# An attention-and-GEGLU kernel whose plan is made by its own list scheduler: DMA transposes before the normalisation, a model of the VectorE–GpSimd port, and another rule for a spare PSUM bank

## The chip, the cores and the metric

The kernel runs on one core of a Trainium2 chip. The metric is device time in microseconds (us), the median of several executions. Engines are called PE (TensorE; PEld is its weight load), ACT (ScalarE), DVE (VectorE), POOL (GpSimd) and SP (SyncE, which here only issues DMAs).

## The reference

```python
x = A_x                                   # 1 x 2048 x 640, bfloat16
h  = x + attention(layernorm(x))          # 32 heads of 20; one shared K and V head; softmax; output weights
h2 = h + geglu(layernorm(h))              # 640 -> 1536 (gate, up) -> 640, tanh gelu
```

Attention over 2048 keys for 32 heads is 2048 score tiles of 128 keys by 512 query columns, each of which needs an exponential. That is the bulk of the work; the rest ("side jobs") is projections, layer norms and the feed-forward part.

## The kernel before

When the kernel is built, a scheduler in Python (the "planner") simulates the five engines with a modelled cost for every operation, and commits each operation to its engine's in-order stream. On the chip only the order and the semaphores remain. So a modelled cost is not a time; it changes the order.

Score tiles are made four at a time (a "pack"; 512 packs). Each tile sits in one PSUM bank until an exponential has read it. ACT computes most exponentials: one 128x512 instruction for a single tile, or one 128x1024 for a pair in adjacent banks. DVE computes the others with an integer trick: one tensor_scalar from PSUM to `pd`, then two shifted copies, which are integer adds of SBUF data, mostly on POOL. A DVE tile thus needs three P·V matmuls instead of one. For each pack the planner chooses how many of the four tiles, `n`, go to DVE: usually one, sometimes two.

```python
    def score_banks():                       # banks 0..5 are for scores; one of 6, 7 holds the P.V sum,
        res = [0, 1, 2, 3, 4, 5]             # the other serves side jobs
        if spare_ok():
            res += [b for b in (6, 7) if bank_owner[b] is None or bank_owner[b] == "s"]
        return res

    def spare_ok():
        us = open_units()
        if not us or active or any(u["acc"] is None for u in us) or len(us) > 1:
            return False
        if len(us[-1]["left"]) < 3:
            return False
        return not state["misc_ready"]

    # issue_qk: how many tiles of this pack go to VectorE
        elif Dv > TH0:
            n = 0
        elif Dv < TH2 or (SP2 and Dv < SP2D and len(pend[1]) + len(pend[2]) < 2 * SP2P
                          and stall(t, 1, fb) + 1382.0 - stall(t, 2, fb) - 956.0 > SP2G):
            n = 2
        else:
            n = 1
```

`Dv` is the work waiting for DVE. `stall(t, n, fb)` estimates how long ACT will wait for the next pack; it counts the banks that `score_banks()` calls free. The constants 1382 and 956 are ACT's modelled time for a pack with one and with two tiles on DVE: a pair and a single, or two singles.

After each of 32 "units" of attention, the sum is copied to `osb`, transposed by PE with an identity matrix, and normalised by DVE:

```python
    def on_job(u, so):
        ...                                  # four matmuls with the identity into a side bank
        def then(b):
            ...
            dve(lambda e: e.reciprocal(rcp..., v5[:, :, :, Dh]), 200, ...)            # from PSUM
            dve(... e.tensor_tensor(o, v5[:, js, :, 0:Dh], rv..., ALU.mult) ...)      # from PSUM, mostly two of them
```

`plan.commit` knows dependences and engine streams, and nothing of a port that two engines share. Its costs before: 635 ns and 1200 ns for POOL's single and double shift, and 420 ns for the layer-norm scaling (`xn_tmp`) on DVE.

The softmax here doesn't subtract the row's maximum and nothing guards it: scores larger than these inputs give would overflow.

Of the kernel before, what the change touches and what calls it, by code (L numbers as in the profile page):

```python
# [4 lines left out]
ALU = mybir.AluOpType  # L5
# [33 lines left out]
class _Plan:  # L39
# [4 lines left out]
    def __init__(self):  # L44
        self.ops = {e: [] for e in self.ENGINES}
        self.free = {e: 0.0 for e in self.ENGINES}
        self.w = {}
        self.r = {}
# [28 lines left out]
    def commit(self, eng, fn, cost, lat, reads=(), writes=(), at=0.0, dma=False):  # L77
        deps = self._deps(eng, reads, writes)
        t0 = max([self.free[eng], at] + [o.vis for o in deps])
        op = _Op(eng, fn, deps, t0, t0 + cost, t0 + cost + lat, dma)  # L80
# [81 lines left out]
class _Task:  # L162


    __slots__ = ("engs", "fn", "cost", "lat", "reads", "writes", "prio", "then", "gate", "born")

    def __init__(self, engs, fn, cost, lat, reads, writes, prio, then=None, gate=None):
# [8 lines left out]
        self.gate = gate  # L176

# [17 lines left out]
def bass_sequential_preLN__grouped_kv_mqa__glu_gated_geglu__prompt_kernel(  # L195
# [33 lines left out]
    LN2G = CHUNKS  # L229
    PE_T1 = (0, 1)  # L230
    PE_T2 = (15,)
    PE_TO = (15,)
    NA = 16
# [29 lines left out]
    osb = sb("osb", [P, 2, 512], BF16)  # L263
    rcp = sb("rcp", [P, 2, 16], F32)
# [50 lines left out]
    POOL_ADD = 635.0  # L315
    POOL_ADD2 = 1200.0
# [16 lines left out]
    NP0 = 4  # L333
    WQA = 1
# [44 lines left out]
    slots = {"xt": list(range(NXT)), "q": list(range(NQ)), "onT": list(range(4)), "osb": [0, 1], "rcp": [0, 1]}  # L379
# [26 lines left out]
    def ln_group(ln, tiles, prio, done):  # L406
# [27 lines left out]
        def norm(t):  # L434
# [33 lines left out]
            tk = _Task(("dve",), None, 420, L_DVE, keys + [("lr", kk)], [], prio, then, gate)  # L468
# [157 lines left out]
    def on_job(u, so):  # L626
        tl, gs = u["tiles"], u["groups"]
        nt, G = len(tl), len(gs)
        pieces = []
        for j in range(4):  # L630
            pieces.append((mm((lambda j: lambda b: ps[:, b * 512 + j * P:b * 512 + (j + 1) * P])(j),
                              osb[:, so, j * P:(j + 1) * P], ident[:], True, True), c_mm(128),
                           [("osb", so), "ident"]))

        def then(b):
            slots["osb"].append(so)
            sr = slots["rcp"].pop(0)
            v5 = bank(b).rearrange("p (j r e) -> p j r e", j=4, r=4)

            def c1(op):  # L640
                cnt = [0]
                parts = []
                rv = rcp[:, sr, :].rearrange("p (j r) -> p j r", j=4)
                if nt == 4:
                    g = gs[0]
                    o = onq[:, onslot[tl[0]]:onslot[tl[0]] + 4, 4 * Dh * g:4 * Dh * (g + 1)].rearrange(
                        "p j (r d) -> p j r d", r=4)
                    parts.append((o, slice(0, 4)))
                elif nt == 2:
                    for gi, g in enumerate(gs):  # L650
                        o = onq[:, onslot[tl[0]]:onslot[tl[0]] + 2, 4 * Dh * g:4 * Dh * (g + 1)].rearrange(
                            "p j (r d) -> p j r d", r=4)
                        parts.append((o, slice(2 * gi, 2 * gi + 2)))
                else:
                    o = onq[:, onslot[tl[0]], 4 * Dh * gs[0]:4 * Dh * (gs[-1] + 1)].rearrange(
                        "p (j r d) -> p j r d", j=4, r=4)
                    parts.append((o, slice(0, 4)))

                def c2(op):
                    cnt[0] += 1  # L660
                    if cnt[0] == len(parts):
                        free_bank(b)
                        slots["rcp"].append(sr)
                        unit_normed(u)

# [47 lines left out]
    def wo_job(t, s, h):  # L713
# [5 lines left out]
        def then(b):  # L719
# [5 lines left out]
            def fin(op):  # L725
                free_bank(b)
                ln_half(1, t, h, 4.0 if t < 12 else 0.7, ln2_after[t])
# [60 lines left out]
    def gate_job(b, fc):  # L788
# [4 lines left out]
        def then(bk):  # L793
            def fin(op):
# [3 lines left out]
                if gate_left[b] == 0:  # L798
                    gelu(b)
# [922 lines left out]
```

## Time and profile before

| | before |
|---|---|
| median | 804.31 us of three runs; 805.01 over six |
| ACT busy | 750.6 us, 93% |
| exponential tiles on ACT / DVE | 1461 / 587 |
| ACT: exponentials, and its idle time just before them | 699.4 + 26.2 us |

The page's first part of the kernel before: busy time of each engine, share of the span, instructions.

```profile
span 804.6 us, 29858 instructions
## 1 busy us (share of the span) xinstructions
PE 693.7 (86%) x13162; PEld 332.3 (41%) x13162; DVE 627.2 (78%) x1156; ACT 750.6 (93%) x1065; POOL 586.2 (73%) x624
```

ACT is nearest to full. Where it is full shows in the table of stretches (busy us of each engine between two times of the execution, with instruction counts):

```profile
...
core 0: us, PE busy (x) PEld busy (x) DVE busy (x) ACT busy (x) POOL busy (x), PEclk, DMA share, GB/s
0.00:25.00 25.00, 13.13 (x286) 8.26 (x286) 20.03 (x72) 15.48 (x25) 11.94 (x35) 1.00 0.71 174
...
105.00:705.00 600.00, 529.85 (x10345) 250.40 (x10343) 475.08 (x836) 583.96 (x824) 455.26 (x457) 0.97 0.06 13
...
770.00:810.00 40.00, 31.63 (x502) 23.89 (x498) 16.47 (x33) 14.84 (x22) 9.14 (x10) 0.98 0.05 18
```

From 105 to 705 us ACT is busy 583.96 of 600 us. Its idle time lies at both ends.

The groups of instructions that matter (line, engine, operation, output <- input, shapes, count; then busy us and mean ns of one; then idle time of that engine just before them, and what ended it):

```profile
...
L1423 ACT ACTIVATE pa<-ps 128x512 bf16<-128x512 f32 (+1 forms) x1012 | 699.4, 844 | 26.2 <-PE ps L1083 21.5
L1486 POOL TENSOR_TENSOR pd<-pd,shifts 128x512 int32<-128x512 int32 x517 | 534.8, 1043 | 170.5 <-DVE pd L1509 161.1 <-PE ps L510 4.8 <-DVE ln_veb L419 1.4
L1509 DVE TENSOR_SCALAR pd<-ps 128x512 uint16<-128x512 f32 x587 | 395.3, 687 | 142.3 <-PE ps L1083 131.3
...
L1466 DVE TENSOR_SCALAR pd<-pd 128x512 uint16<-128x512 uint16 (+2 forms) x66 | 37.8, 595 | 0.0
...
L472 DVE TENSOR_SCALAR xn_tmp<-xh,mv,ln_r 128x640 bf16<-128x640 bf16 x32 | 21.4, 686 | 0.4
...
L668 DVE TENSOR_TENSOR onq<-ps,rcp 128x160 bf16<-128x160 f32 (+1 forms) x60 | 18.0, 329 | 0.8
...
L674 DVE RECIPROCAL rcp<-ps 128x16 f32<-128x16 f32 x32 | 8.0, 249 | 8.1 <-PE ps L510 6.6 <-PE ps L506 1.3
```

The first line split by form (its busy times add up records that overlap each other):

```profile
...
L1423 ACT ACTIVATE pa<-ps 128x1024 bf16<-128x1024 f32 x449 | 484.7, 1082 | 2.4 <-PE ps L1083 2.3
L1423 ACT ACTIVATE pa<-ps 128x512 bf16<-128x512 f32 x563 | 354.9, 653 | 23.8 <-PE ps L1083 19.2
```

ACT's 1012 instructions cover 1461 tiles, so 699.4 us is 479 ns per tile on average. DVE has room: it sits idle 142.3 us before its exponential tiles. The waits (who waited for whom: us in total, times, longest) show the loop:

```profile
...
PEld ps L1083 <- DVE pd L1509: 161.3, 357, 2.1
POOL pd L1486 <- DVE pd L1509: 161.1, 338, 5.7
DVE pd L1509 <- PE ps L1083: 131.3, 206, 2.5
...
ACT pa L1423 <- PE ps L1083: 21.5, 46, 1.5
```

DVE waits for PE's score matmuls, and the weight loads of score matmuls wait for DVE to give a bank back.

One line from the view of a single source line, for ACT's exponentials (minimum, median and maximum ns; first and last start), is the ruler:

```profile
...
engine op xcount: duration ns min/median/max, first and last start us, forms
L1423 ACT ACTIVATE pa<-ps x1012: 591/756/1242, 14.2 to 777.8; 128x512 bf16<-128x512 f32 x167, 128x1024 bf16<-128x1024 f32 x2
```

The span is 14.2 us before the first exponential, 763.6 us until the last starts, and 804.6 − 777.8 = 26.8 us after that: the tail, which is the feed-forward part of the last rows.

And the same view of the layer-norm scaling:

```profile
...
L472 DVE TENSOR_SCALAR xn_tmp<-xh,mv,ln_r x32: 422/444/1214, 7.1 to 789.1; 128x640 bf16<-128x640 bf16 x32
```

Its median is 444 ns, but some take nearly three times that. The trace shows why: each of the 11 that took over 700 ns and started while a GpSimd operation ran ended 182 to 185 ns after that operation ended, so the long ones had waited it out.

### The profile page before, as it was taken

Reading aid. Unit: us, or ns where it says so; the run is one execution under the profiler, and the core shown is the slowest. Engines: PE = TensorE matmul, PEld = TensorE weight load, DVE = VectorE, ACT = ScalarE, POOL = GpSimd, SP = SyncE. Lnnn points to the kernel's source line nnn. Section 1 sums busy time; section 2 is a strip of 40 time slices with the busy share of each in tenths; the row PEclk is TensorE's granted clock in tenths of the full one; section 3 lists DMA queues with packets and bytes.
Section 4 is the critical chain, followed back from the end, with each engine's and each line's share of the span. In section 5 each row is a group of like instructions: output and inputs, shape, how many; then the busy total and the mean of one; then the engine's idle time right before and its main releaser. Section 6 shows DMA issues by size and latency. Waiting matters only on the chain.

```text
span 804.6 us, 29858 instructions
## 1 busy us (share of the span) xinstructions
PE 693.7 (86%) x13162; PEld 332.3 (41%) x13162; DVE 627.2 (78%) x1156; ACT 750.6 (93%) x1065; POOL 586.2 (73%) x624
## 2 busy tenths in 40 slices
PE   5687778989978998789988799888998899887998
PEld 3332223534434443345433444334444444343457
DVE  7868789877887778877788777988779776877864
ACT  5899999999989999899999999999999999999981
POOL 4587877868767677767878678877777668776760
PEclk9999999989999999999999999999999999998999
DMA  7680001000100000000000000000010000100000
GB/s 198 118 311 2 2 13 24 3 2 2 35 19 3 2 20 18 18 3 3 19 19 18 3 2 19 19 19 2 2 35 19 3 2 19 19 18 11 11 19 18
DMA packets 40288, 21.96 MB, mean 27 GB/s; under 512 B 31328, under 2 KB 38880, under 8 KB 40160
## 3 DMA queue, kind: packets, MB, share of 16 engines
q1 hardware_dynamic: 38848, 19.61, 9.6%
q8 instruction: 105, 1.72, 0.9%
q10 hardware_dynamic: 1312, 0.44, 0.3%
q14 instruction: 23, 0.19, 0.1%
HBM read 10.21 MB, written 2.62 MB: 16 GB/s over the span
## 4 chain that ended last, share of the span: by engine, by line
PE 46%; DVE 25%; ACT 25%; issue 2%; DMA 1%; POOL 1%; POOLq 0%; DVEq 0%
ACT pa L1423 25%; PE ps L510 17%; DVE pd L1509 15%; PE ps L1083 13%; PE ps L1162 13%; DVE pd L1466 3%; PE ps L506 3%; DVE xn_tmp L472 2%; DVE osb L1189 1%; DVE stats L403 1%; DVE qT L580 1%; DVE xh L728 1%; DVE onq L668 1%; DMA onT<-onq 1%; DVE ln_vb L415 0%
## 5 line engine op out<-in xcount | busy, mean ns | idle before, releaser
L1423 ACT ACTIVATE pa<-ps 128x512 bf16<-128x512 f32 (+1 forms) x1012 | 699.4, 844 | 26.2 <-PE ps L1083 21.5
L1486 POOL TENSOR_TENSOR pd<-pd,shifts 128x512 int32<-128x512 int32 x517 | 534.8, 1043 | 170.5 <-DVE pd L1509 161.1
L1509 DVE TENSOR_SCALAR pd<-ps 128x512 uint16<-128x512 f32 x587 | 395.3, 687 | 142.3 <-PE ps L1083 131.3
L1162 PE MATMUL ps<-pd,v_ext 128*32 128x512 bf16 x1761 | 276.2, 400 | 28.0 <-DVE osb L1189 21.5
L1162 PE MATMUL ps<-pa,v_ext 128*32 128x512 bf16 x1461 | 265.4, 393 | 2.7 <-ACT pa L1423 1.3
L1083 PE MATMUL ps<-qT,kT 32*128 32x512 bf16 x2048 | 206.8, 390 | 65.9 <-DVE pd L1509 41.0
L1083 PEld LDWEIGHTS ps<-qT,kT 32*128 32x128 bf16 x2048 | 58.9, 91 | 233.7 <-DVE pd L1509 161.3
L1162 PEld LDWEIGHTS ps<-pd,v_ext 128*32 128x32 bf16 x1761 | 74.8, 98 | 79.1 <-issue 35.0
L1162 PEld LDWEIGHTS ps<-pa,v_ext 128*32 128x32 bf16 x1461 | 70.6, 96 | 43.1 <-issue 30.3
L510 PE MATMUL ps<-xn2T,wg_sb 128*32 128x256 bf16 (+1 forms) x1720 | 66.1, 278 | 0.1
L510 PE MATMUL ps<-xn2T,wu_sb 128*32 128x256 bf16 x1680 | 64.9, 276 | 0.5 <-DVE onq L668 0.4
L510 PE MATMUL ps<-wd_sb,gbuf 128*32 128x320 bf16 x1344 | 64.4, 301 | 0.2 <-DVE onq L668 0.2
L510 PE MATMUL ps<-xn1T,wq_pad 128*32 128x256 bf16 (+1 forms) x1440 | 51.0, 267 | 0.2
L510 PEld LDWEIGHTS ps<-xn2T,wu_sb 128*32 128x32 bf16 x1680 | 42.9, 97 | 18.7 <-issue 10.3
L510 PEld LDWEIGHTS ps<-xn2T,wg_sb 128*32 128x32 bf16 x1720 | 42.1, 98 | 17.6 <-issue 11.5
L510 PEld LDWEIGHTS ps<-wd_sb,gbuf 128*32 128x32 bf16 x1344 | 33.5, 96 | 23.8 <-issue 11.8
L510 PEld LDWEIGHTS ps<-xn1T,wq_pad 128*32 128x32 bf16 x1440 | 33.8, 98 | 13.8 <-issue 8.9
L846 DVE TENSOR_TENSOR gbuf<-ps,gbuf 128x512 bf16<-128x512 f32 x48 | 32.9, 685 | 6.6 <-PE ps L506 6.4
L1466 DVE TENSOR_SCALAR pd<-pd 128x512 uint16<-128x512 uint16 (+2 forms) x66 | 37.8, 595 | 0.0
L1472 POOL TENSOR_TENSOR pd<-pd,shifts 128x256 int32<-128x256 int32 x48 | 30.2, 635 | 3.9 <-DVE pd L1509 3.4
L403 DVE BATCH_NORM_STATS2 stats<-xh 128x6 f32<-128x320 bf16 x64 | 29.9, 477 | 1.3 <-DMA xh<-in_A_x_dram 1.1
L809 DVE CAST gbuf<-ps 128x512 bf16<-128x512 f32 x42 | 28.7, 683 | 1.0 <-PE ps L510 0.9
(71 smaller groups left out, 357.8 us busy)
## 6 DMA issues: line engine op xcount, KB each, us to landing
out_dram<-xh SPq DMA_DIRECT2D x16, 160.0 KB, 1.8
xh<-in_A_x_dram SPq DMA_DIRECT2D x3, 640.0 KB, 6.3
wg_sb<-in_B_w_gate_dram SPq DMA_DIRECT2D x1, 1920.0 KB, 9.3
wu_sb<-in_B_w_up_dram SPq DMA_DIRECT2D x1, 1920.0 KB, 13.6
wd_sb<-in_B_w_down_dram SPq DMA_DIRECT2D x1, 1920.0 KB, 18.0
wo_sb<-in_A_wo_dram SPq DMA_DIRECT2D x1, 800.0 KB, 5.5
gbuf<-in_A_wq_dram ACTq DMA_DIRECT2D x1, 400.0 KB, 4.6
gbuf<-in_A_wq_dram SPq DMA_DIRECT2D x1, 400.0 KB, 6.9
```

The lines of the kernel that those rows point to most:

```text
L403: dve(lambda e: e.bn_stats(stats[:, ln, t, 6 * h:6 * h + 6], xh[:, t, h * HALF:(h + 1) * HALF]), 395, [key], [("st", ln, t, h)], prio, c)
L506: return e.matmul(o(b), l, r, start=st, stop=sp)
L510: ins = e.matmul(o(b)[a, :], l[:, a], r, start=st, stop=sp, tile_position=(0, 32 * j))
L809: dve(lambda e: e.tensor_copy(o, i), c_dve(n * k), [("b", bk)], ks, 1.0, fin)
L846: dve(lambda e: e.tensor_tensor(o, i, o, ALU.mult), c_dve(n * k), [("b", bk)] + ks, ks, 1.0, fin)
L1083: ins = e.matmul(bank(b), kT4[32 * r:32 * r + 32, kt * P:(kt + 1) * P], qT[32 * r:32 * r + 32, s, :], start=True, stop=True, tile_position ...
L1162: ins = e.matmul(ps[32 * r:32 * r + 32, ab * 512:(ab + 1) * 512], v_ext[:, it["kt"], it["w"], :], it["ap"], start=st, stop=(j in ends), ti ...
L1423: op = plan.commit("act", lambda e: e.activation(dst, src, ACT.Exp, scale=SM_SCALE), cost, L_ACT, [("b", b0 + i) for i in range(n)], [("pa ...
L1466: return e.tensor_scalar(pd[:, w, a], pd[:, 0, a], float(CH_SHIFT[w]), None, ALU.add)
L1472: return e.tensor_tensor(pd32[:, w, h], pd32[:, 0, h], shifts[:, w - 1:w].to_broadcast([P, 256 * k]), ALU.add)
L1486: return e.tensor_tensor(pd32[:, 1:3, h], pd32[:, 0, h].unsqueeze(1).to_broadcast([P, 2, 256]), shifts[:].unsqueeze(2).to_broadcast([P, 2, ...
L1509: op = plan.commit("dve", lambda e: e.tensor_scalar(pd[:, 0, s * 512:(s + 1) * 512], bank(b), CH_A, CH_B, ALU.mult, ALU.add), c_dve(512), ...
```

## The change

The intent has three parts: take the transposes and products of the normalisation off PE and DVE; tell the planner that VectorE and GpSimd can lock each other out; and let score tiles use a seventh bank more often. The diff, cut to its core:

```diff
     def commit(self, eng, fn, cost, lat, reads=(), writes=(), at=0.0, dma=False, lock=False):
         t0 = max([self.free[eng], at] + [o.vis for o in deps])
+        if lock:                                   # a VectorE op that takes the port
+            for o in self.ops["pool"][-2:]:
+                if o.t0 <= t0 < o.end:
+                    t0 = o.end
+            self.port = t0 + cost
+        elif eng == "pool":
+            t0 = max(t0, self.port)
...
-    POOL_ADD = 635.0
-    POOL_ADD2 = 1200.0
+    POOL_ADD = 580.0
+    POOL_ADD2 = 1010.0
...
-            tk = _Task(("dve",), None, 420, L_DVE, keys + [("lr", kk)], [], prio, then, gate)
+            tk = _Task(("dve",), None, 320, L_DVE, keys + [("lr", kk)], [], prio, then, gate)
+            tk.lock = True                         # layer-norm scaling; VectorE's shifts are marked too
...
     # normalisation: units 30 and 31 still go through PE; the other 30:
+            tk.fn = lambda e: e.dma_start_transpose(onr[:, s, :].rearrange("p (j i) -> p j i", j=4), osb[:, so, :])
+        # then the reciprocal on DVE from onr, and the product as one instruction:
+            if key[0] == "b":
+                dve(fn, 400, [key, ("rcp", sr)], ks, 0.9, c2)
+            else:
+                task(("pool",), fn, POOL_NM, L_POOL, [key, ("rcp", sr)], ks, 0.9, c2)
...
     def spare_ok():
-        us = open_units()
-        if not us or active or any(u["acc"] is None for u in us) or len(us) > 1:
-            return False
-        if len(us[-1]["left"]) < 3:
-            return False
-        return not state["misc_ready"]
+        if active or state["misc_ready"]:
+            return False
+        us = open_units()
+        if SPK == 0:                               # the old rule
+            return bool(us) and len(us) == 1 and us[0]["acc"] is not None and len(us[-1]["left"]) >= 3
+        if state["kv_left"] > 0 or not any(u["acc"] is not None for u in us):
+            return False
+        return SPK == 1 or len(us[-1]["left"]) != 16      # SPK is 1
...
-        cost, lat = (k * 512 / (1.92 if POOL_ADD else 3.84) + 72.0, L_DVE) if eng == "dve" else (POOL_ADD, L_POOL)
+        cost, lat = (k * 512 / 3.84 + 72.0, L_DVE) if eng == "dve" else (POOL_ADD, L_POOL)
...
+            if tk.lock and plan.free["pool"] > t + LOCKW:          # VectorE holds such an op back
+                continue
...
+        if YIELD and state["kv_left"] == 0 and plan.free["dve"] < t + YIELD:   # POOL yields to such an op
+            ...
```

The product's move needs its input in SBUF, and the DMA transpose puts it there: the Trainium skill ("GPSIMD Engine Reference", Engine selection) says that GpSimd has no PSUM port.

More of the change, by code (lines that the diff above doesn't have):

```diff
@@ L46, in __init__ @@
         self.free = {e: 0.0 for e in self.ENGINES}
+        self.port = 0.0
         self.w = {}
@@ L75, in ready, with commit @@
         return t
-    def commit(self, eng, fn, cost, lat, reads=(), writes=(), at=0.0, dma=False):
+    def commit(self, eng, fn, cost, lat, reads=(), writes=(), at=0.0, dma=False, lock=False):
         deps = self._deps(eng, reads, writes)
         t0 = max([self.free[eng], at] + [o.vis for o in deps])
+        if lock:
[5 more added lines that the diff above has]
+            t0 = max(t0, self.port)
         op = _Op(eng, fn, deps, t0, t0 + cost, t0 + cost + lat, dma)
@@ L162 @@
 class _Task:
-    __slots__ = ("engs", "fn", "cost", "lat", "reads", "writes", "prio", "then", "gate", "born")
+    __slots__ = ("engs", "fn", "cost", "lat", "reads", "writes", "prio", "then", "gate", "born", "lock")
     def __init__(self, engs, fn, cost, lat, reads, writes, prio, then=None, gate=None):
@@ L176, in __init__ @@
         self.gate = gate
+        self.lock = False
 class _Job:
@@ L229, in bass_sequential_preLN__grouped_kv_mqa__glu_gated_geglu__prompt_kernel @@
     LN2G = CHUNKS
+    MERGE = [(i,) for i in range(9)]
     PE_T1 = (0, 1)
@@ L232, in bass_sequential_preLN__grouped_kv_mqa__glu_gated_geglu__prompt_kernel @@
     PE_TO = (15,)
+    PE_ON = (30, 31)
+    POOL_NM = 750.0
     NA = 16
@@ L263, in bass_sequential_preLN__grouped_kv_mqa__glu_gated_geglu__prompt_kernel @@
     osb = sb("osb", [P, 2, 512], BF16)
+    onr = sb("onr", [P, 2, 512], BF16)
     rcp = sb("rcp", [P, 2, 16], F32)
@@ L333, in bass_sequential_preLN__grouped_kv_mqa__glu_gated_geglu__prompt_kernel @@
     NP0 = 4
+    LNT = 12
+    SPK = 1
+    LOCKW = 200.0
+    YIELD = 700.0
     WQA = 1
@@ L378, in bass_sequential_preLN__grouped_kv_mqa__glu_gated_geglu__prompt_kernel @@
     bank_owner = {b: None for b in range(8)}
-    slots = {"xt": list(range(NXT)), "q": list(range(NQ)), "onT": list(range(4)), "osb": [0, 1], "rcp": [0, 1]}
+    slots = {"xt": list(range(NXT)), "q": list(range(NQ)), "onT": list(range(4)), "osb": [0, 1], "rcp": [0, 1], "onr": [0, 1]}
     pa_free = [True] * NA
@@ L624, in q_job, with normed @@
         jobs.append(jb)
-    def on_job(u, so):
+    def normed(u, so, v, key, done):
         tl, gs = u["tiles"], u["groups"]
         nt, G = len(tl), len(gs)
-        pieces = []
-        for j in range(4):
-            pieces.append((mm((lambda j: lambda b: ps[:, b * 512 + j * P:b * 512 + (j + 1) * P])(j),
-                              osb[:, so, j * P:(j + 1) * P], ident[:], True, True), c_mm(128),
-                           [("osb", so), "ident"]))
-        def then(b):
-            slots["osb"].append(so)
-            sr = slots["rcp"].pop(0)
-            v5 = bank(b).rearrange("p (j r e) -> p j r e", j=4, r=4)
-            def c1(op):
-                cnt = [0]
-                parts = []
-                rv = rcp[:, sr, :].rearrange("p (j r) -> p j r", j=4)
-                if nt == 4:
-                    g = gs[0]
-                    o = onq[:, onslot[tl[0]]:onslot[tl[0]] + 4, 4 * Dh * g:4 * Dh * (g + 1)].rearrange(
-                        "p j (r d) -> p j r d", r=4)
-                    parts.append((o, slice(0, 4)))
-                elif nt == 2:
-                    for gi, g in enumerate(gs):
-                        o = onq[:, onslot[tl[0]]:onslot[tl[0]] + 2, 4 * Dh * g:4 * Dh * (g + 1)].rearrange(
-                            "p j (r d) -> p j r d", r=4)
-                        parts.append((o, slice(2 * gi, 2 * gi + 2)))
-                else:
-                    o = onq[:, onslot[tl[0]], 4 * Dh * gs[0]:4 * Dh * (gs[-1] + 1)].rearrange(
-                        "p (j r d) -> p j r d", j=4, r=4)
-                    parts.append((o, slice(0, 4)))
-                def c2(op):
-                    cnt[0] += 1
-                    if cnt[0] == len(parts):
-                        free_bank(b)
-                        slots["rcp"].append(sr)
-                        unit_normed(u)
-                for o, js in parts:
-                    nj = js.stop - js.start
-                    dve((lambda o, js, nj: lambda e: e.tensor_tensor(
-                        o, v5[:, js, :, 0:Dh], rv[:, js, :].unsqueeze(3).to_broadcast([P, nj, 4, Dh]), ALU.mult))(
-                            o, js, nj), c_dve(80 * nj), [("b", b), ("rcp", sr)],
-                        [("onq", onslot[t], g) for t in tl for g in (gs if nj == 4 else [gs[js.start // 2]])],
-                        0.9, c2)
-            dve(lambda e: e.reciprocal(rcp[:, sr, :].rearrange("p (j r) -> p j r", j=4), v5[:, :, :, Dh]), 200,
-                [("b", b)], [("rcp", sr)], 0.8, c1)
@@ L677, in gate, with bind, c1, c2 @@
+        v4 = v.rearrange("p (j r e) -> p j r e", j=4, r=4)
         def gate():
             return bool(slots["rcp"]) and all(x in on_sent for t in tl for x in on_before[t])
-        jobs.append(_Job(("on", u["id"]), 1.5, pieces, then, gate))
+        sl = []
+        def bind():
+            sr = slots["rcp"].pop(0)
+            sl.append(sr)
+            tk.writes = [("rcp", sr)]
+            tk.fn = lambda e: e.reciprocal(rcp[:, sr, :].rearrange("p (j r) -> p j r", j=4), v4[:, :, :, Dh])
+        def c1(op):
+            sr = sl[0]
+            o = onq[:, onslot[tl[0]]:onslot[tl[0]] + nt, 4 * Dh * gs[0]:4 * Dh * (gs[-1] + 1)]
+            o = o.rearrange("p t (g r d) -> p g t r d", g=G, r=4)
+            i0 = v4[:, :, :, 0:Dh].rearrange("p (g t) r d -> p g t r d", g=G)
+            i1 = rcp[:, sr, :].rearrange("p (g t r) -> p g t r", g=G, t=nt).unsqueeze(4).to_broadcast(
+                [P, G, nt, 4, Dh])
+            def c2(op):
+                slots["rcp"].append(sr)
+                done()
+                unit_normed(u)
+            fn = (lambda e: e.tensor_tensor(o, i0, i1, ALU.mult))
+            ks = [("onq", onslot[t], g) for t in tl for g in gs]
+            if key[0] == "b":
+                dve(fn, 400, [key, ("rcp", sr)], ks, 0.9, c2)
+            else:
+                task(("pool",), fn, POOL_NM, L_POOL, [key, ("rcp", sr)], ks, 0.9, c2)
@@ new lines, in normed, with on_job, then, bind @@
+        tk = _Task(("dve",), None, 120, L_DVE, [key], [], 0.8, c1, gate)
+        tk.born = bind
+        tasks.append(tk)
+    def on_job(u, so):
+        if u["id"] in PE_ON:
+            pieces = []
+            for j in range(4):
+                pieces.append((mm((lambda j: lambda b: ps[:, b * 512 + j * P:b * 512 + (j + 1) * P])(j),
+                                  osb[:, so, j * P:(j + 1) * P], ident[:], True, True), c_mm(128),
+                               [("osb", so), "ident"]))
+            def then(b):
+                slots["osb"].append(so)
+                normed(u, so, bank(b), ("b", b), lambda: free_bank(b))
+            jobs.append(_Job(("on", u["id"]), 1.5, pieces, then,
+                             lambda: all(x in on_sent for t in u["tiles"] for x in on_before[t])))
+            return
+        tk = _Task(("sp",), None, 1330, 1500, [("osb", so)], [], 0.5, None, lambda: bool(slots["onr"]))
+        sl = []
+        def bind():
+            s = slots["onr"].pop(0)
+            sl.append(s)
+            tk.writes = [("onr", s)]
+            tk.fn = lambda e: e.dma_start_transpose(onr[:, s, :].rearrange("p (j i) -> p j i", j=4), osb[:, so, :])
+        def sent(op):
+            s = sl[0]
+            slots["osb"].append(so)
+            normed(u, so, onr[:, s, :], ("onr", s), lambda: slots["onr"].append(s))
+        tk.born = bind
+        tk.then = sent
+        sp_tasks.append(tk)
@@ L726, in fin @@
                 free_bank(b)
-                ln_half(1, t, h, 4.0 if t < 12 else 0.7, ln2_after[t])
+                ln_half(1, t, h, 4.0 if t < LNT else 0.7, ln2_after[t])
             dve(lambda e: e.tensor_tensor(xh[:, t, h * HALF:(h + 1) * HALF], xh[:, t, h * HALF:(h + 1) * HALF],
@@ L797, in fin @@
                 copied[b].append(fc)
-                if gate_left[b] == 0:
-                    gelu(b)
+                gated(b)
             def fin2(op):
@@ L804, in fin2 @@
                 up_job(b, fc)
-                if gate_left[b] == 0 and copied[b]:
-                    gelu(b)
+                gated(b)
             o, i = gview(b, fc, k), bview(bk, b, k)
@@ L813, in gate_job, with gated @@
         jobs.append(_Job(("gate", b, fc), 5.0, gu_pieces(wg_sb, b, fc), then, lambda: g_free(b)))
+    def gated(b):
+        grp = next(m for m in MERGE if b in m)
+        if all(gate_left[x] == 0 for x in grp):
+            for x in grp:
+                if copied[x]:
+                    gelu(x)
     def gelu(b):
@@ L885, in bass_sequential_preLN__grouped_kv_mqa__glu_gated_geglu__prompt_kernel @@
     for gl in LN2G:
-        aft = ln_group(1, gl, 4.0 if gl[0] < 12 else 0.7, x2_done)
+        aft = ln_group(1, gl, 4.0 if gl[0] < LNT else 0.7, x2_done)
         for t in gl:
@@ L1382, in run_task @@
                 cost += 1283.0
-        op = plan.commit(eng, tk.fn, cost, lat, tk.reads, tk.writes, at=t)
+        op = plan.commit(eng, tk.fn, cost, lat, tk.reads, tk.writes, at=t, lock=tk.lock)
         if tk.then:
@@ L1473, in fn @@
                                        shifts[:, w - 1:w].to_broadcast([P, 256 * k]), ALU.add)
-        op = plan.commit(eng, fn, cost, lat, [("pd", 0, s0 + i) for i in range(k)] + [("sh", w)], [("pd", w, s0 + i) for i in range(k)], at=t)
+        op = plan.commit(eng, fn, cost, lat, [("pd", 0, s0 + i) for i in range(k)] + [("sh", w)], [("pd", w, s0 + i) for i in range(k)], at=t, lock=eng == "dve")
         for x in recs:
@@ L1574, in pool_decide @@
     def pool_decide(t):
+        if YIELD and state["kv_left"] == 0 and plan.free["dve"] < t + YIELD:
+            for tk in tasks:
+                if tk.lock and known(tk) and (tk.gate is None or tk.gate()) and plan.ready(
+                        "dve", tk.reads, tk.writes) <= t + YIELD:
+                    return False
         best = None
```

## The prediction

> **What bounds the kernel now.** The page's busy table: ScalarE (ACT) 750.6 of 804.6 us (93%), PE 86%, VectorE (DVE) 78%, GpSimd (POOL) 73%. Busy time by stretch: from 105 to 705 us ACT is busy 584 of 600 us; its idle time lies in the first and last 25 us. So only work taken off ACT shortens the middle. That work is 699 us of exponentials (groups of instructions): 1461 score tiles of 128x512, 479 ns each. DVE does the other 587 tiles (687 ns as recorded). DVE idles 131 us before those, waiting for score matmuls, and weight loads of score matmuls wait 161 us (the waits) for DVE to free a PSUM bank: the six score banks are a closed loop. That is why the planner rarely gives DVE two of a pack's four tiles (587 over 512 packs), though DVE has time.
>
> **What the change does.**
> 1. For 30 of 32 units the transpose before normalisation goes from PE to a DMA, the product from DVE to POOL. Off PE: 480 small matmuls, about 0.41 us per unit in the timeline, 12 us. Off DVE: a reciprocal of 249 ns and two products of 317 ns per unit, 26 us; a reciprocal of about 0.17 us returns (estimate from the 142 ns one of 128x2), so 20 us net. On POOL: 30 products of about 0.75 us (estimate from the 635 ns 128x256 add), 23 us. This kernel's DMA transposes land in 2.6 to 2.9 us, hidden except at a chunk's end. A side bank, held 1.6 us per unit, comes free.
> 2. Port model. The layer-norm scaling on DVE (xn_tmp) has a median of 444 ns but a mean of 686; the shifts on DVE (pd from pd) run 276 to 1257 ns. The Trainium skill ("SBUF — State Buffer", Who interferes with whom) says a VectorE op in a 2-port mode and a GpSimd op lock each other out for a whole instruction; these spreads agree with waiting out a 1043 ns POOL add. At most 8 us (norms) plus 16 us (shifts) of DVE is there to win; I count a third. POOL pays with some idle time.
> 3. Spare bank. Now allowed only with a single open unit and three packs left; then whenever no side job is active or ready. A seventh bank loosens the loop, so more packs give DVE two tiles. Most of the gain comes from here; 1 and 2 make room on DVE.
>
> **Sum.** 25 to 30 us of DVE time freed, plus part of its 131 us of waiting: I expect 50 (20 to 90) more tiles on DVE, 637. Each takes 479 ns off ACT: 24 us less. PE gains 0.11 us per tile (two more P·V tiles, four abreast) and loses 12 us: even. POOL gets 50 x 1.04 + 23 = 75 us more, about 660 of 785: close, not the limit. ACT's idle time may grow a few us; head and tail stay.
>
> Predicted: **783 us**, range 769 to 799. Faster by over 2%: 0.65; within 2%: 0.32; slower: 0.03.
>
> **What would show it.** Exponentials on DVE 610 to 680; on ACT busy 665 to 690 us; ACT above 96% busy in the middle; weight loads of score matmuls waiting on DVE below 130 us; xn_tmp mean below 600 ns; 30 onq products on POOL of 0.6 to 1.0 us; POOL 80 to 87%.
>
> **What would make it wrong.** Tiles on DVE stay near 590: then only a few us (step 3 fails). POOL becomes late with products, yields and shifts: pd buffers run out and PE waits for POOL. Score tiles in the spare bank delay side jobs: the tail grows. The planner's order fits the chip worse: ACT idles.

## The result, and the profile after

| | before | after |
|---|---|---|
| median of six runs each, us | 805.01 | 793.82 (791.72 to 795.87) |
| ratio | | 0.9863 (95%: 0.9845 to 0.9881) |
| exponential tiles on DVE | 587 | 602 |
| exponentials on ACT + idle before them, us | 699.4 + 26.2 | 691.5 + 21.9 |
| tail after the last ACT exponential starts, us | 26.8 | 27.2 |

A ratio is the mean time of one kernel's fast runs over that of the other's fast runs in the same rounds, so it is not quite the ratio of the medians.

The time fell by 1.4%: inside the predicted range, but about half of the 21 us that were expected. The same views of the kernel after (line numbers moved with the change: L1423 is now L1466, L1509 is L1552, L472 is L491). The busy table:

```profile
span 793.7 us, 29128 instructions
## 1 busy us (share of the span) xinstructions
PE 689.3 (87%) x12779; PEld 324.2 (41%) x12779; DVE 618.0 (78%) x1128; ACT 741.5 (93%) x1059; POOL 617.1 (78%) x673
```

The stretches:

```profile
...
core 0: us, PE busy (x) PEld busy (x) DVE busy (x) ACT busy (x) POOL busy (x), PEclk, DMA share, GB/s
0.00:25.00 25.00, 14.58 (x306) 9.45 (x310) 19.13 (x69) 13.62 (x19) 11.98 (x35) 0.93 0.64 173
...
105.00:705.00 600.00, 530.10 (x10105) 244.30 (x10109) 477.42 (x829) 586.89 (x836) 484.46 (x503) 0.99 0.10 19
...
770.00:810.00 40.00, 20.93 (x290) 18.23 (x287) 10.00 (x22) 4.19 (x7) 0.56 (x1) 1.00 0.04 14
```

ACT is still full in the middle, 586.89 of 600 us; the execution just ends earlier. The groups:

```profile
...
L1466 ACT ACTIVATE pa<-ps 128x512 bf16<-128x512 f32 (+1 forms) x1010 | 691.5, 843 | 21.9 <-PE ps L1126 18.3 <-PE ps L1205 0.4
L1529 POOL TENSOR_TENSOR pd<-pd,shifts 128x512 int32<-128x512 int32 x521 | 535.8, 1041 | 114.4 <-DVE pd L1552 109.7 <-DVE ln_veb L437 1.7 <-DVE ln_vb L433 1.4
L1552 DVE TENSOR_SCALAR pd<-ps 128x512 uint16<-128x512 f32 x602 | 404.4, 687 | 140.0 <-PE ps L1126 130.4
...
L1509 DVE TENSOR_SCALAR pd<-pd 128x512 uint16<-128x512 uint16 (+1 forms) x77 | 38.9, 517 | 0.0
...
L674 POOL TENSOR_TENSOR onq<-onr,rcp 128x320 bf16<-128x320 bf16 x30 | 21.9, 730 | 16.6 <-DVE rcp L660 16.5
...
L491 DVE TENSOR_SCALAR xn_tmp<-xh,mv,ln_r 128x640 bf16<-128x640 bf16 x32 | 19.2, 609 | 0.1
...
L660 DVE RECIPROCAL rcp<-onr 128x16 f32<-128x16 bf16 x30 | 7.4, 246 | 5.3 <-DMA onr<-osb 5.3
```

The waits:

```profile
...
PEld ps L1126 <- DVE pd L1552: 139.1, 349, 1.4
DVE pd L1552 <- PE ps L1126: 130.4, 219, 2.5
POOL pd L1529 <- DVE pd L1552: 109.7, 255, 3.1
...
ACT pa L1466 <- PE ps L1126: 18.3, 45, 1.6
```

The ruler, and the layer-norm scaling:

```profile
...
engine op xcount: duration ns min/median/max, first and last start us, forms
L1466 ACT ACTIVATE pa<-ps x1010: 591/747/1242, 14.8 to 766.5; 128x512 bf16<-128x512 f32 x166, 128x1024 bf16<-128x1024 f32 x3
```

```profile
...
L491 DVE TENSOR_SCALAR xn_tmp<-xh,mv,ln_r x32: 397/445/1278, 6.9 to 777.2; 128x640 bf16<-128x640 bf16 x32
```

Add it up along ACT, between the two profiled executions (804.6 and 793.7 us, a difference of 10.9). The first exponential starts 0.6 us later. Exponentials take 7.9 us less, ACT's idle time before them is 4.3 us less, ACT's other work and idle time is about the same, and the tail is 0.4 us longer. So about two thirds of the gain is less exponential work on ACT and one third is less waiting. By form ACT has 13 pairs fewer and 11 singles more (436 and 574, shown below); at the 904 and 478 ns that the second round reads from the traces, that is 6.5 of the 7.9 us. The prediction wanted 24 us from the first and no gain from the second.

The room on DVE was made, and was not used: DVE spent 9.1 us more on 15 more tiles, yet its busy time fell from 627.2 to 618.0 us, and its idle time waiting for score matmuls stayed (131.3, now 130.4 us).

### The profile page after: what moved, and what is told of

Same layout as the page of the kernel before. It is cut to its first block, busy times and chain, and to the rows that moved or that the text cites. A ratio compares the mean times of both kernels' runs of the same rounds, so it can differ in the third digit from the quotient of the medians.

```text
span 793.7 us, 29128 instructions
## 1 busy us (share of the span) xinstructions
PE 689.3 (87%) x12779; PEld 324.2 (41%) x12779; DVE 618.0 (78%) x1128; ACT 741.5 (93%) x1059; POOL 617.1 (78%) x673
## 4 chain that ended last, share of the span: by engine, by line
ACT 42%; PE 38%; DVE 12%; DMA 4%; issue 2%; POOL 1%
ACT pa L1466 38%; PE ps L529 14%; PE ps L1126 11%; PE ps L1205 10%; DVE pd L1552 7%; PE ps L525 3%; ACT gbuf L870 2%; DMA onr<-osb 2%; DVE osb L1232 1%; DVE xn_tmp L491 1%; ACT L1466 1%; ACT L870 1%; DMA xh<-in_A_x_dram 1%; POOL pd L1529 1%; DVE pd L1509 1%
## 5 line engine op out<-in xcount | busy, mean ns | idle before, releaser
L1466 ACT ACTIVATE pa<-ps 128x512 bf16<-128x512 f32 (+1 forms) x1010 | 691.5, 843 | 21.9 <-PE ps L1126 18.3
L1552 DVE TENSOR_SCALAR pd<-ps 128x512 uint16<-128x512 f32 x602 | 404.4, 687 | 140.0 <-PE ps L1126 130.4
L1205 PE MATMUL ps<-pa,v_ext 128*32 128x512 bf16 x1446 | 258.4, 390 | 1.8 <-ACT pa L1466 1.4
L1126 PE MATMUL ps<-qT,kT 32*128 32x512 bf16 x2048 | 205.7, 389 | 60.1 <-DVE pd L1552 35.8
L1126 PEld LDWEIGHTS ps<-qT,kT 32*128 32x128 bf16 x2048 | 58.5, 91 | 226.4 <-DVE pd L1552 139.1
L1205 PEld LDWEIGHTS ps<-pa,v_ext 128*32 128x32 bf16 x1446 | 67.3, 95 | 43.8 <-issue 25.6
L529 PE MATMUL ps<-wd_sb,gbuf 128*32 128x320 bf16 x1340 | 68.8, 301 | 0.5 <-DVE gbuf L887 0.5
L529 PE MATMUL ps<-xn2T,wg_sb 128*32 128x256 bf16 x1680 | 63.8, 275 | 1.4 <-DVE gbuf L843 1.0
L529 PEld LDWEIGHTS ps<-xn2T,wg_sb 128*32 128x32 bf16 x1680 | 41.2, 97 | 20.0 <-issue 10.9
L1515 POOL TENSOR_TENSOR pd<-pd,shifts 128x256 int32<-128x256 int32 x63 | 40.9, 658 | 1.4 <-DVE pd L1552 1.4
L1509 DVE TENSOR_SCALAR pd<-pd 128x512 uint16<-128x512 uint16 (+1 forms) x77 | 38.9, 517 | 0.0
L674 POOL TENSOR_TENSOR onq<-onr,rcp 128x320 bf16<-128x320 bf16 x30 | 21.9, 730 | 16.6 <-DVE rcp L660 16.5
```

The costliest lines, as they stand in the source:

```text
L529: ins = e.matmul(o(b)[a, :], l[:, a], r, start=st, stop=sp, tile_position=(0, 32 * j))
L1126: ins = e.matmul(bank(b), kT4[32 * r:32 * r + 32, kt * P:(kt + 1) * P], qT[32 * r:32 * r + 32, s, :], start=True, stop=True, tile_position ...
L1205: ins = e.matmul(ps[32 * r:32 * r + 32, ab * 512:(ab + 1) * 512], v_ext[:, it["kt"], it["w"], :], it["ap"], start=st, stop=(j in ends), ti ...
L1466: op = plan.commit("act", lambda e: e.activation(dst, src, ACT.Exp, scale=SM_SCALE), cost, L_ACT, [("b", b0 + i) for i in range(n)], [("pa ...
L1509: return e.tensor_scalar(pd[:, w, a], pd[:, 0, a], float(CH_SHIFT[w]), None, ALU.add)
L1515: return e.tensor_tensor(pd32[:, w, h], pd32[:, 0, h], shifts[:, w - 1:w].to_broadcast([P, 256 * k]), ALU.add)
```

## The experiments

Twelve kernels ran besides the change, each with three timed rounds against the kernel before on the same chip, and all gave correct results. Counts of tiles per bank are counted in the kernel's own plan, not in the trace. The three rounds ran on three different chips, where the median of the kernel before was 806.16, 806.21 and 805.03 us, so kernels of different rounds are best compared by their ratios. The table holds all of them; the columns after the ratio are read from each run's profile (groups, and the first and last start of ACT's exponentials).

| run | ratio to before (95%) | median us | tiles on DVE | ACT exponentials + idle before, us | tail, us |
|---|---|---|---|---|---|
| the change | 0.9863 (0.9845–0.9881) | 793.82 | 602 | 691.5 + 21.9 | 27.2 |
| a_spare_old | 0.9963 (0.9936–0.9991) | 803.38 | 583 | 698.7 + 21.1 | 27.4 |
| a_pe_on | 1.0013 (0.9983–1.0043) | 807.52 | 597 | 696.2 + 31.1 | 26.7 |
| a_port_off | 0.9973 (0.9943–1.0004) | 803.30 | 618 | 687.5 + 33.1 | 31.8 |
| a_neutral | 0.9832 (0.9797–0.9867) | 791.72 | 616 | 687.2 + 23.4 | 27.3 |
| a_view_only | 0.9914 (0.9873–0.9954) | 799.33 | 606 | 691.2 + 25.1 | 27.3 |
| a_place_only | 0.9895 (0.9872–0.9918) | 797.94 | 594 | 694.7 + 22.5 | 27.2 |
| a_dve800 | 0.9909 (0.9886–0.9933) | 798.66 | 650 | 677.5 + 29.9 | 33.9 |
| a_sp2g0 | 1.0064 (1.0044–1.0084) | 811.11 | 679 | 670.5 + 50.2 | 41.9 |
| a_spare_old_n | 0.9864 (0.9842–0.9885) | 794.49 | 596 | 693.1 + 18.4 | 27.2 |
| a_dma_dve | 1.0012 (0.9983–1.0040) | 805.77 | 612 | 690.4 + 32.1 | 27.2 |
| a_lock_only_off | 1.0164 (1.0145–1.0183) | 818.50 | 630 | 685.5 + 43.4 | 31.6 |
| a_no_fill | 0.9862 (0.9818–0.9906) | 793.11 | 613 | 688.8 + 26.5 | 27.2 |

### First round: undo one part at a time, and a change that means nothing

**a_spare_old**: the old spare-bank rule in the changed kernel.

```diff
-    SPK = 1
+    SPK = 0
```

> The changed kernel with the old spare-bank rule alone put back. The built program has 583 exponential tiles on VectorE, against 602 after and 587 before, and places 58 score tiles in banks 6 and 7, against 62 after and 29 before. Theory S (the prediction: the spare-bank rule brings most of the gain, through more tiles on VectorE): 801 to 806 us, ScalarE exponentials back at about 699 us. Rival N (taking the normalisation off PE, VectorE and the side bank brings the gain, whatever the rule): 792 to 797 us.

It measured 803.38 us, as theory S wanted. Taken alone it says that the rule is worth some 10 us. That does not hold up; see a_spare_old_n.

**a_pe_on**: all 32 transposes before the normalisation on PE again, product on DVE from PSUM.

```diff
-    PE_ON = (30, 31)
+    PE_ON = tuple(range(32))
```

> The changed kernel with all 32 transposes before the normalisation back on PE (and the product back on VectorE, as one instruction a unit); new rule and port model stay. 597 exponential tiles on VectorE, 33 score tiles in banks 6 and 7. Theory S: the tiles on VectorE stay near 602, so 793 to 798 us. Rival N: 800 to 806 us, nearly all of the gain gone, although the tile count hardly moves; PE's idle before score matmuls and their weight loads grows, since the side bank is held again.

It measured 807.52 us: the whole gain is gone although DVE has 597 tiles. ACT's idle time before exponentials is 31.1 us instead of 21.9:

```profile
...
L1466 ACT ACTIVATE pa<-ps 128x512 bf16<-128x512 f32 (+1 forms) x1011 | 696.2, 832 | 31.1 <-PE ps L1126 25.9
```

The time lies just above theory N's 800 to 806 us. One sign that N gave is not there: PE's idle time before score matmuls fell, from 60.1 to 49.5 us, and that before their weight loads from 226.4 to 210.6.

**a_port_off**: no lock, no holding back, no yielding, and the old costs.

```diff
-            tk.lock = True                 # and lock=eng == "dve" in the shifts' commit
+            tk.lock = False
-    POOL_ADD = 580.0
-    POOL_ADD2 = 1010.0
+    POOL_ADD = 635.0
+    POOL_ADD2 = 1200.0
...                                         # scaling 320 -> 420, shifts 3.84 -> 1.92 elements per ns
```

> The changed kernel with the port model and the new costs of shifts and scaling taken out (old costs back). 618 exponential tiles on VectorE. If the port model is worth what the prediction gave it, about 8 us of VectorE time and so 3 to 4 us in all: 796 to 799 us, xn_tmp mean back to about 690 ns. If it is worth nothing: 792 to 795 us. If the count of tiles on VectorE alone set the time (0.479 us each), the 16 extra tiles would give 786 us.

It measured 803.30 us, 9.5 us above the change, although ACT has 4 us less to do: idle time before exponentials grew by 11.2 us and the tail by 4.6 us:

```profile
...
L1466 ACT ACTIVATE pa<-ps 128x1024 bf16<-128x1024 f32 (+1 forms) x1009 | 687.5, 825 | 33.1 <-PE ps L1126 27.3 <-PE ps L1205 1.1
```

That is more than the 3 to 4 us that were expected for the part, but it is one order, and no larger than what a meaningless nudge did in a_spare_old_n. The scaling's mean was 653 ns, not back at the expected 690. The count of tiles does not set the time.

**a_neutral**: one modelled cost nudged.

```diff
-    POOL_NM = 750.0
+    POOL_NM = 760.0
```

> The changed kernel with one modelled cost (the GpSimd product) at 760 instead of 750 ns: no cause, only another order. It measures how far the plan's order alone moves the time. The program has 616 exponential tiles on VectorE. If the tile count alone set the time: 787 us. If not: 791 to 797 us, and differences below about 3 us between the other variants are not to be read.

It measured 791.72 us. Its ratio and that of the change have overlapping intervals. Fourteen more tiles on DVE brought nothing that can be told from noise.

### Second round: how does the rule act, and what are more tiles on DVE worth?

**a_view_only** and **a_place_only** split the rule. `score_banks()` feeds both the placing of tiles and the planner's estimate of stalls.

```diff
 # a_view_only: tiles are placed by the old rule (spare_old), the estimate uses the new one
-        return sorted(b for r, b in res if r <= t + 30), res
+        return sorted(b for r, b in res if r <= t + 30 and (b < 6 or spare_old())), res
 # a_place_only: tiles are placed by the new rule, the estimate uses the old one
-        free += [r for r, b in free_banks(t)[1] if b not in fb]
+        free += [r for r, b in free_banks(t)[1] if b not in fb and (b < 6 or spare_old())]
```

> The changed kernel; score tiles are placed in banks 6 and 7 by the old rule, but the planner's estimate of ScalarE's coming wait (which decides between one and two tiles for VectorE) counts those banks as free by the new rule. 606 exponential tiles on VectorE, 52 score tiles in banks 6 and 7. Theory P (the seventh bank itself helps, by holding more score tiles): the gain of the rule is lost, 800 to 804 us. Rival V (the rule works through the planner's view: it makes the planner hand VectorE more second tiles, while the bank itself is hardly used): 792 to 797 us, as the changed kernel.

> The changed kernel; score tiles are placed in banks 6 and 7 by the new rule, but the estimate that decides between one and two tiles for VectorE counts those banks by the old rule. 594 exponential tiles on VectorE, 58 score tiles in banks 6 and 7. Theory P: 792 to 797 us. Rival V: 799 to 804 us, ScalarE exponentials about 696 us.

They measured 799.33 and 797.94 us: both between the expectations, and alike. The two theories are not told apart here.

**a_dve800** and **a_sp2g0** make the planner give DVE more second tiles.

```diff
-    SP2D = 400.0                            # a_dve800
+    SP2D = 800.0
-    SP2G = 300.0                            # a_sp2g0
+    SP2G = 0.0
```

> The changed kernel with the limit on VectorE's waiting work for a second tile at 800 instead of 400 ns: 650 exponential tiles on VectorE against 602. If the count of tiles taken off ScalarE sets the time, as the prediction's sum had it (0.479 us each): 48 tiles give 771 us. Rival C (the score banks are a closed loop; a second tile on VectorE keeps a bank longer, and ScalarE then waits for score matmuls): ScalarE exponentials do fall to about 668 us, but the idle time before them grows from 22 to 40 us or more, and the time is 793 to 803 us.

> The changed kernel with the threshold on the estimated gain of a second VectorE tile at 0 instead of 300 ns: 679 exponential tiles on VectorE, 28 score tiles in banks 6 and 7. By the tile count alone: 757 us. By rival C: ScalarE exponentials about 654 us, idle before them 60 us or more, time 800 to 815 us.

They measured 798.66 and 811.11 us. The times lie in rival C's ranges, but its forecasts for ACT were too strong: exponentials of about 668 and 654 us (measured 677.5 and 670.5), and 40 and 60 us or more of idle time (29.9 and 50.2). That a second tile on DVE holds a bank longer was not tested by itself. The profiles show three separate costs. The groups by form of the change (first) and of a_dve800 (second); the busy column here adds up records that overlap each other, so only the counts are used:

```profile
...
L1466 ACT ACTIVATE pa<-ps 128x1024 bf16<-128x1024 f32 x436 | 472.5, 1086 | 2.8 <-PE ps L1126 2.8
L1466 ACT ACTIVATE pa<-ps 128x512 bf16<-128x512 f32 x574 | 360.3, 657 | 19.1 <-PE ps L1126 15.5 <-PE ps L1205 0.4
```

```profile
...
L1466 ACT ACTIVATE pa<-ps 128x1024 bf16<-128x1024 f32 x389 | 404.2, 1043 | 2.5 <-PE ps L1126 1.4 <-PE ps L1205 1.1
L1466 ACT ACTIVATE pa<-ps 128x512 bf16<-128x512 f32 x620 | 365.5, 625 | 27.4 <-PE ps L1126 19.4 <-PE ps L1205 0.4
```

First, the price per tile. The 48 tiles broke up 47 pairs: 436 and 574 became 389 and 620. ACT's exponential time fell from 691.5 to 677.5 us, 14.0 us, which is 0.29 us per tile and not the average 0.479. A tile that leaves a pair leaves a single behind. A least-squares fit of the exponential time of all 14 profiles to their counts of pairs and singles gives 864 ns for a pair and 551 ns for a single (an estimate), so 0.31 us for a tile that leaves a pair. The traces separate two parts of this. Where the next instruction on ACT starts before the record of an exponential ends, it starts 904 ns (median) after a pair started and 478 ns after a single, before, after and in a_dve800: back to back, a tile that leaves a pair saves 426 ns. The Trainium skill ("ScalarE: Activation LUTs", What ACT_TABLE_LOAD costs) gives 0.833 ns per element, so 427 ns for 512 more elements, an estimate with which that agrees. The rest of the saving is lost where ACT has nothing to do next: then the whole record, at least 591 ns for a single, counts as busy. Singles followed by such a gap are 98 in a_dve800, against 47 after the change.

Second, the idle time before ACT's exponentials grew by 8.0 us in a_dve800 and by 28.3 us in a_sp2g0. Third, the tail. The ruler of a_dve800:

```profile
...
L1466 ACT ACTIVATE pa<-ps x1009: 591/653/1192, 13.2 to 761.5; 128x1024 bf16<-128x1024 f32 x105, 128x512 bf16<-128x512 f32 x64
```

The last exponential starts 5.0 us earlier than after the change, but the span ends at 795.4 us, a tail of 33.9 us instead of 27.2. In the groups of that stretch PE still had 132 up-projection matmuls and 96 down-projection matmuls to do, against 120 and 61 after the change (222 and 96 in a_sp2g0). That side work had been left behind while the attention ran. PE's busy time rose by 7.5 us over the change, which fits the extra P·V work of the tiles; that this is what pushed the side jobs back was not tested by itself.

### Third round: is the rule's loss real, and what do the two other parts rest on?

**a_spare_old_n**: a_spare_old with the nudge of a_neutral.

```diff
-    SPK = 1
-    POOL_NM = 750.0
+    SPK = 0
+    POOL_NM = 760.0
```

> The kernel of the first run (changed kernel, old spare-bank rule) with the neutral nudge of the fourth (modelled GpSimd product 760 instead of 750 ns). 596 exponential tiles on VectorE against 583 without the nudge. If the first run's loss of about 10 us was the rule's: 801 to 805 us again. If it was partly the luck of one order: 794 to 799 us, and single removals are then known to no better than about 5 us.

It measured 794.49 us, ratio 0.9864: with the old rule the kernel is as fast as the change (0.9863). Its groups:

```profile
...
L1466 ACT ACTIVATE pa<-ps 128x512 bf16<-128x512 f32 (+1 forms) x1010 | 693.1, 856 | 18.4 <-PE ps L1126 14.9 <-PE ps L1205 0.2
...
L1552 DVE TENSOR_SCALAR pd<-ps 128x512 uint16<-128x512 f32 x596 | 401.0, 688 | 151.3 <-PE ps L1126 141.3
```

596 tiles on DVE, and ACT idle only 18.4 us before its exponentials. The fair partner of this run is a_neutral, which has the same nudge and the new rule: 791.72 against 794.49 us, with overlapping intervals of the ratio. So of two pairs of orders one gives the rule 9.6 us and the other 2.8 us, and the rule's share cannot be told from the luck of an order; that it is zero is not shown either. What is shown is that nearly the whole gain can be had without the rule, and that the rule hardly changes the use of the bank: 62 of 2048 tiles in the plan of the change, 58 and 60 with the old rule, 29 in the kernel before. The run also gives a yardstick: a meaningless nudge moved the kernel with the old rule by 8.9 us (8 us by the ratios). One order without a part, compared with one order with it, can mislead by about that much.

**a_dma_dve**: DMA transposes stay, but the product is on DVE, from SBUF.

```diff
-            if key[0] == "b":
+            if True:
                 dve(fn, 400, [key, ("rcp", sr)], ks, 0.9, c2)
```

> The changed kernel with the product back on VectorE, from the SBUF buffer that the DMA transpose fills; PE and the side bank stay relieved. 612 exponential tiles on VectorE. Theory B (the relief of PE and of the side bank is what the new normalisation brings): 791 to 797 us. Rival D (the product's time off VectorE is what it brings): 799 to 806 us, since VectorE gets about 30 times 0.4 us back and GpSimd loses 22 us.

It measured 805.77 us: the gain is gone, with PE and the side bank still relieved. The time lies where rival D put it and not where theory B did. But theory B is not ruled out by this, because the experiment did more than move the work. The product's line in a_dma_dve, and the same product from PSUM in a_pe_on:

```profile
...
L674 DVE TENSOR_TENSOR onq<-onr,rcp x30: 468/574/1335, 59.3 to 738.6; 128x320 bf16<-128x320 bf16 x30
```

```profile
...
L674 DVE TENSOR_TENSOR onq<-ps,rcp x32: 480/491/492, 59.7 to 783.4; 128x320 bf16<-128x320 f32 x32
```

From PSUM every one takes 480 to 492 ns. From SBUF the range is 468 to 1335 ns, and the group's mean is 799. The Trainium skill ("SBUF — State Buffer", Who interferes with whom) says that a VectorE instruction with two SBUF inputs contends with a GpSimd instruction that reads SBUF; this spread agrees, and the trace shows the wait itself: all 18 that took 553 ns or more started while a GpSimd add ran and ended 346 to 350 ns after it ended. In a_pe_on 24 of the 32 started beside a GpSimd operation too, and none was longer than 492 ns. The planner did not know it: it planned 400 ns and no lock. So POOL is not only the less busy engine for this product; on DVE from SBUF it ran into POOL's adds. On POOL the product takes 0.73 us (21.9 us for 30).

**a_lock_only_off**: the corrected costs stay, the lock goes.

```diff
-            tk.lock = True                 # and lock=eng == "dve" in the shifts' commit
+            tk.lock = False
```

> The changed kernel with the port lock, VectorE's holding back and GpSimd's yielding taken out of the planner, but the corrected costs of adds, shifts and scaling kept. 630 exponential tiles on VectorE. Theory L (the lock model is what made the port part worth about 10 us): 800 to 806 us. Rival K (the corrected costs are, as the shifts on VectorE then go from 120 back to about 77 instructions): 792 to 797 us.

It measured 818.50 us, 13 us slower than the kernel before and 25 us slower than the change. That is far more than the yardstick, and more than theory L expected. Its groups:

```profile
...
L1466 ACT ACTIVATE pa<-ps 128x512 bf16<-128x512 f32 (+1 forms) x1012 | 685.5, 805 | 43.4 <-PE ps L1126 34.0 <-PE ps L1205 3.2
...
L1509 DVE TENSOR_SCALAR pd<-pd 128x512 uint16<-128x512 uint16 (+1 forms) x65 | 40.8, 657 | 0.0
...
L491 DVE TENSOR_SCALAR xn_tmp<-xh,mv,ln_r 128x640 bf16<-128x640 bf16 x32 | 20.9, 674 | 0.2
```

ACT's idle time doubled, 43.4 against 21.9 us. DVE's single shifts average 543 ns against 490 after the change, the double ones 828 against 591, and the scaling 674 against 609. With the corrected costs and no lock the plan holds these operations to be short and free of waiting; on the chip they are not. That ACT's idle time comes from what stands behind the late ones in DVE's stream is argued, not shown. The old cost of POOL's double add (1200 ns) was too high: adds that follow each other directly start 997 ns apart in the trace, and the new cost is 1010. So the old costs left slack; that this is why they do less harm (a_port_off) is argued from the planner, not shown.

**a_no_fill**: without the matmuls on zeros that fill quiet stretches of PE.

```diff
-    QUIET = 0.5
+    QUIET = 0.0
```

> The changed kernel without the matmuls on zeros that fill quiet stretches of PE (156 in the changed kernel, 56 before). 613 exponential tiles on VectorE. If the 100 extra fill matmuls cost the changed kernel part of the expected gain: 789 to 792 us. If they run in time that PE had free: 792 to 796 us, with the granted clock as before (0.97 to 0.99).

It measured 793.11 us, ratio 0.9862: the 100 extra fill matmuls after the change cost nothing that can be seen. The granted clock of its four runs was 0.959 to 0.974, below the 0.981 to 0.991 of the change's runs and no higher than the 0.968 to 0.977 of the kernel before in the experiments' rounds. So the change's higher clock is not what made it faster; a_port_off had 0.987 to 0.991 and lost nearly all of the gain.

No version clearly beats the change: a_neutral is 2.1 us faster in the median, with overlapping intervals.

## Why the prediction was right or wrong

- **What bounds the kernel: right, but not complete.** ACT is full in the middle before and after, and the gain can be added up along ACT. But ACT's idle time before exponentials is as movable as its work: over the 14 profiles it lies between 18.4 and 50.2 us, and, with the tail, it decides between a_dve800, a_sp2g0, a_port_off and a_lock_only_off.
- **Step 1, the normalisation: right in its terms, too small in its role.** DVE lost 26.0 us of reciprocals and products (8.0 + 18.0) and kept 8.9 (32 reciprocals and two products), so 17 us net against 20 predicted; the reciprocal from SBUF takes 246 ns, not the estimated 170. POOL got 21.9 us against 23. The prediction treated this as making room for more DVE tiles. In a_pe_on and a_dma_dve the gain is gone when PE or DVE gets the work back, at 597 and 612 tiles. Those are single orders, and their losses (12 us each by the ratios) exceed the yardstick of 8 us, but not by much.
- **Step 2, the port: right about the size that it named, wrong about what it is good for.** The scaling's mean fell from 686 to 609 ns (missing the predicted 600) and the double shifts on DVE fell from 737 to 591; with the single ones that is about 6 us of DVE time (32 × 0.077 + 20 × 0.146 + 56 × 0.012), near the third of 24 us that was counted. The mean of the scaling varies between orders, though: 546 to 658 ns in the kernels with the lock, 653 and 674 in the two without it. For the order the lock matters more: the time grows by 25 us when it goes and the corrected costs stay. That is the harm of half a model and not the worth of the whole part, which a_port_off puts at 9.5 us, no clearer than the yardstick.
- **Step 3, the spare bank: this is the step that failed.** "A seventh bank loosens the loop, so more packs give DVE two tiles. Most of the gain comes from here; 1 and 2 make room on DVE." The seventh bank is hardly used (62 of 2048 tiles, 58 without the rule), DVE got 15 more tiles instead of 50, its wait for score matmuls stayed (131.3, now 130.4 us), and nearly the whole gain is still there without the rule in one of two orders (a_spare_old_n). The loop was not loosened; why the planner does not use the bank more was not asked.
- **The term that was mis-sized even if the tiles had come: "Each takes 479 ns off ACT".** That is the average cost of a tile. The tiles that move come out of pairs, and a_dve800 measured 0.29 us each, with 8.0 us of idle time and 6.7 us of tail against it. Forty-eight more tiles did not make the kernel 23 us faster than the change; it was 4.8 us slower, which is within the yardstick. With 77 more (a_sp2g0) it was 17 us slower, which is not.
- **The total: the range of 769 to 799 held, the most likely class did not.** The time fell by 1.4%, while "faster by over 2%" had been given 0.65. That the range held is in part luck: the step that was to bring most of the gain did not happen, and a third of the gain came from less waiting, which the sum had not counted. The signs that the prediction named show it too: exponentials on DVE 602 (610 to 680 predicted) and 691.5 us on ACT (665 to 690), weight loads waiting 139.1 us for DVE (below 130), POOL at 78% (80 to 87%). The 30 products on POOL at 0.73 us and ACT's 98% in the middle came as predicted, but ACT had 97% there before, so this last sign says little.

What stays open: how the 11 us divide between the normalisation, the port model and, within the noise of orders, the rule. With either of them undone, in whole or in half, nearly all of it is lost (ratios 0.9973 to 1.0164 in those four kernels, 0.9832 to 0.9963 in the seven orders that have both and the change's thresholds), so they do not simply add, and no kernel here has only one of them on top of the kernel before. Even this border is thin: the intervals of a_port_off (0.9943 to 1.0004) and of a_spare_old (0.9936 to 0.9991), which has both parts, overlap. The kernel before is also a single order and was never nudged, so how much of the 11 us is its bad luck or the change's good luck is not known; the mean ratio of the seven orders is 0.9885. The split of the rule (view against placing) was not decided.

## What to carry to other kernels

Price moved work at the margin, not at the average: a tile that leaves a paired instruction saved 0.43 us back to back and 0.29 us of busy time in a_dve800, where the average tile cost 0.48 us, and the wait and the backlog that it left behind took that back. When a kernel's order comes from a scheduler with modelled costs, run a meaningless nudge beside every ablation, because one order can be 9 us away from its neighbour and look like a cause. And correct a scheduler's costs only together with the waits that the old costs had swallowed: right durations without the port lock made this kernel slower than the wrong ones did.

## What the Trainium skill lacked or had wrong

- "SBUF — State Buffer", Who interferes with whom: it states that the shared port blocks for a whole instruction, and the runs agree, but it gives no sizes for such forms. Here the 128x640 bfloat16 scaling on VectorE took 397 ns at best and 1278 at worst beside GpSimd adds of 1039 ns (median); the 128x320 product with two SBUF inputs took 468 to 1335 ns, the long ones ending 346 to 350 ns after the add that they had waited for, against 480 to 492 ns from PSUM.
- "GPSIMD Engine Reference", Elementwise — side-by-side cycle accounting: it has the time of a tensor_tensor of float32, and none of a 32-bit integer add with a broadcast input. Here that took a median of 614 ns for 128x256 and 1039 ns for 128x512, so 1.66 ns for each further element (425 / 256); the 128x320 bfloat16 product took 728 ns.
- "Perfetto Trace Analysis", Optimizing Scalar/DVE Operations: it gives VectorE a smaller overhead on SBUF than on PSUM (about 60 against 125 ns, as engine-busy time, with about twice that in a profiled instruction). The recorded time of the 128x16 reciprocal does not show it: 249 ns from PSUM (float32), 246 from SBUF (bfloat16).
- No page has the time to landing of an SBUF-to-SBUF DMA transpose of this size: here 2.6 us (median) for 128x512 bfloat16.
